# A gated linear recurrence with a causal convolution behind it: 1024-token chunks, word transposes, another split of the engines, and an order written out in full

## The chip, the cores and the metric

The kernel runs on one core of one Trainium2 chip. The metric is the device time of a run in microseconds; the figure for the kernel before is the median of three runs. Besides these runs there is one profiled execution of it, from which every duration below comes.

## What is computed

The inputs `x`, `r_gate` and `i_gate` are float32 of 4 x 6336 x 256 (batch, time, channel). The reference, cut to what matters:

```python
a_base = 1 / (1 + exp(-a_param))
sig_r, sig_i = sigmoid(r_gate), sigmoid(i_gate)
a_t = exp(8.0 * sig_r * log(clip(a_base, 1e-6, 1 - 1e-6)))
x_gated = sqrt(maximum(1 - a_t * a_t, 1e-6)) * sig_i * x
for t in range(S):                       # a recurrence along time, per channel
    h = a_t[:, t] * h + x_gated[:, t]
    y[:, t] = h
gate_pre = sum(conv_w[k] * y_shifted_by(4 - k) for k in range(5))   # causal, per channel
out = (sigmoid(gate_pre) * (y @ w_val)) @ w_out                     # 256 x 256 weights
```

The output is float32, 4 x 6336 x 256. In all, 104 MB go over the DMA queues.

## The kernel before

The 25,344 tokens are cut into windows of 512 (the last has 256). For each window, three loads on SP's queue bring r, i and x in token order (tokens on the partitions, 256 channels in each row; a partition gets four rows of 1 KB that lie 128 tokens apart). The window then passes through these steps; L numbers are lines of the kernel before:

- `tanh` (ACT, L240) makes tanh(r/2) and tanh(i/2), both gates in one instruction, into `tri`, in bf16. Sigmoids are expressed by tanh.
- `u2` (DVE, L246) makes (tanh + 1) * x, the gated input without the norm, into `uring`, still in token order.
- `srT` (PE, L228) transposes the r gate in bf16 blocks of 128 x 128, so that channels lie on the partitions and time runs along the columns. `exp` (ACT, L257, once for each half h of the channels) turns it into a_t in `aring`.
- `e` (POOL, L262) squares a_t into `ering`. `sq` (ACT, L277) takes the square root for several windows at once, since the square root lives in another activation table than tanh and exp; each change costs an ACT_TABLE_LOAD.
- `uT` (PE, L228) transposes the gated input, `xg` (DVE, L290) multiplies it by the norm, in channel order, from PSUM and SBUF into SBUF.
- `scan` (DVE, L306) runs the recurrence along 512 columns for each h into `yring`; POOL copies the last four columns of the window before in front of it (L304), for the convolution.
- `conv` (PE, L321) is a matmul with a diagonal 128 x 128 matrix for each of five taps and two halves; `tg` (ACT, L327) its tanh; `val` (PE, L338) is y @ w_val; `gv` (DVE, L344) makes (tg + 1) * val; `out` (PE, L356) multiplies by w_out, back in token order; `osb` copies PSUM to SBUF on DVE (L367) or ACT (L369); `store` writes out from SP's queue (L373).

The order of issue comes from `make_plan`, a planner that holds a cost and a priority for each step, places each step on its engine at the earliest time that its inputs allow, and sorts the steps by that time. Each engine then executes its instructions in that order, and SP its loads and stores in that order: a store that waits for its copies holds the loads behind it. Buffers: three windows of input, eleven of a_t, squares and u, seven of y. PSUM holds two banks' worth each of `gp` and `val`, and smaller tiles for the transposes and the output.

## Time and profile before

| quantity | value |
|---|---|
| median of 3 runs | 376.22 us (373.58 to 376.86) |
| span of the profiled execution, first to last instruction | 372.5 us |
| mean granted TensorE clock | 0.942 |
| busy: DVE / ACT / PE / POOL | 334.6 / 312.4 / 272.4 / 138.3 us |
| moved by DMA | 104.42 MB, mean 280 GB/s |
| packets between 512 B and 2 KB | nearly all of 105,160 |
| table loads on ACT | 27 of 1.283 us |

The page gives no time of the profiled execution beside its span; the difference to the median, 3.7 us, is what lies around the span. A busy share is the time in which an engine has an instruction under way, averaged over the whole span, so it has to be read by stretches. A group's line names the source line, the engine, the operation, output and input tiles with their sizes, the number of instructions, their busy time, the mean duration in ns, and the idle time of the engine just before them, with what ended it. An idle engine costs something only where others wait for it.

### The profile page before, as it was taken

Reading aid. Unit: us, or ns where it says so; the run is one execution under the profiler, and the core shown is the slowest. Engines: PE = TensorE matmul, PEld = TensorE weight load, DVE = VectorE, ACT = ScalarE, POOL = GpSimd, SP = SyncE. Lnnn points to the kernel's source line nnn. Section 1 sums busy time; section 2 is a strip of 40 time slices with the busy share of each in tenths; the row PEclk is TensorE's granted clock in tenths of the full one; section 3 lists DMA queues with packets and bytes.
Section 4 is the critical chain, followed back from the end, with each engine's and each line's share of the span. In section 5 each row is a group of like instructions: output and inputs, shape, how many; then the busy total and the mean of one; then the engine's idle time right before and its main releaser. Section 6 shows DMA issues by size and latency. Waiting matters only on the chain.

```text
span 372.5 us, 5299 instructions
## 1 busy us (share of the span) xinstructions
PE 272.4 (73%) x1933; PEld 159.9 (43%) x1933; DVE 334.6 (90%) x326; ACT 312.4 (84%) x298; POOL 138.3 (37%) x111
## 2 busy tenths in 40 slices
PE   0362779877686969877677887696976696869994
PEld 0232445444445535434344454363543363435543
DVE  3363999999999979999999999999999999999982
ACT  4898899999998799998967989789997997873342
POOL 2234435634362726434425324451655056300000
PEclk9995699999899899999889989789999899999998
DMA  8999996999999989996889979979999895313333
GB/s 210 355 348 353 356 350 201 298 353 339 345 361 324 330 268 361 352 364 202 280 264 339 351 226 295 356 255 344 301 323 336 278 340 187 127 56 114 113 114 141
DMA packets 105160, 104.42 MB, mean 280 GB/s; under 512 B 3240, under 2 KB 105135, under 8 KB 105135
## 3 DMA queue, kind: packets, MB, share of 16 engines
q1 hardware_dynamic: 104590, 103.83, 85.7%
q0 software_dynamic: 544, 0.26, 0.5%
q8 instruction: 15, 0.25, 0.3%
q14 instruction: 11, 0.08, 0.1%
HBM read 78.39 MB, written 25.95 MB: 280 GB/s over the span
## 4 chain that ended last, share of the span: by engine, by line
DVE 34%; ACT 23%; issue 19%; PE 14%; DMA 5%; POOL 2%; DVEq 0%; ACTq 0%
DVE yring L306 13%; DVE uring L246 8%; DVE gv L344 7%; ACT tri L240 6%; ACT ering L277 5%; PE gp L321 5%; PE ops L356 4%; ACT aring L257 4%; DMA xt<-in_x_dram 3%; DVE xg L290 3%; PE val L338 3%; ACT tg L327 3%; DVE osb L367 2%; ACT L327 2%; ACT L277 2%
## 5 line engine op out<-in xcount | busy, mean ns | idle before, releaser
L262 POOL TENSOR_TENSOR ering<-aring 128x1024 f32<-128x1024 f32 (+1 forms) x50 | 105.7, 2121 | 140.9 <-ACT aring L257 121.8
L321 PE MATMUL gp<-yring,diag 128*128 128x512 bf16 (+4 forms) x530 | 124.5, 384 | 24.7 <-DVE yring L306 14.2
L306 DVE TENSOR_TENSOR_SCAN yring<-aring,yring,xg 128x512 bf16<-128x512 f32 (+4 forms) x98 | 139.5, 1464 | 0.7
L240 ACT ACTIVATE tri<-ri 128x2048 bf16<-128x2048 f32 (+1 forms) x50 | 94.4, 1907 | 0.0
L321 PEld LDWEIGHTS <-diag 128*128 128x128 bf16 x530 | 50.8, 102 | 83.5 <-issue 16.3
L356 PE MATMUL ops<-wo,gv 128*128 128x256 bf16 x396 | 61.8, 280 | 26.2 <-DVE gv L344 12.4
L257 ACT ACTIVATE aring<-srT,khf 128x512 f32<-128x512 bf16 (+1 forms) x100 | 71.8, 791 | 3.4 <-PE srT L228 2.2
L246 DVE SCALAR_TENSOR_TENSOR uring<-tri,xt 128x1024 bf16<-128x1024 bf16 (+1 forms) x50 | 67.4, 1356 | 7.0 <-ACT tri L240 6.9
L327 ACT ACTIVATE tg<-gp 128x1024 bf16<-128x1024 f32 (+1 forms) x50 | 51.1, 1023 | 25.7 <-PE gp L321 21.2
L344 DVE SCALAR_TENSOR_TENSOR gv<-tg,val 128x1024 bf16<-128x1024 bf16 (+1 forms) x50 | 59.7, 1194 | 2.5 <-PE val L338 1.7
L304 POOL COPY yring<-yring 128x8 bf16<-128x8 bf16 x49 | 31.6, 644 | 77.4 <-DVE yring L306 77.4
L356 PEld LDWEIGHTS <-gv 128*128 128x128 bf16 x396 | 36.7, 99 | 50.0 <-DVE gv L344 20.2
L338 PE MATMUL val<-yring,wv 128*128 128x512 bf16 (+4 forms) x212 | 52.1, 371 | 5.3 <-DVE gv L344 5.3
L228 PE MATMUL srT<-ident_b,tri 128*128 128x128 bf16 x396 | 33.4, 232 | 22.2 <-ACT tri L240 22.2
L277 ACT ACTIVATE ering<-ering,b 128x3072 bf16<-128x3072 f32 (+2 forms) x21 | 47.0, 2280 | 0.1
L369 ACT COPY osb<-ops 128x512 f32<-128x512 f32 x46 | 27.2, 592 | 22.2 <-PE ops L356 19.1
L367 DVE COPY osb<-ops 128x512 f32<-128x512 f32 x53 | 36.1, 682 | 9.2 <-PE ops L356 8.0
L228 PE MATMUL uT<-ident_b,uring 128*128 128x128 bf16 x396 | 33.3, 232 | 15.0 <-DVE xg L290 14.7
L228 PEld LDWEIGHTS <-tri 128*128 128x128 bf16 x396 | 27.0, 104 | 33.2 <-ACT tri L240 27.1
L290 DVE TENSOR_TENSOR xg<-uT,ering 128x1024 bf16<-128x1024 bf16 (+1 forms) x50 | 33.7, 675 | 6.2 <-ACT ering L277 6.2
L228 PEld LDWEIGHTS <-uring 128*128 128x128 bf16 x396 | 28.3, 104 | 20.0 <-issue 14.3
L338 PEld LDWEIGHTS <-wv 128*128 128x128 bf16 x212 | 19.9, 99 | 18.9 <-issue 6.6
(31 smaller groups left out, 53.3 us busy)
## 6 DMA issues: line engine op xcount, KB each, us to landing
ri<-in_r_gate_dram SPq DMA_DIRECT2D x49, 512.0 KB, 6.1
ri<-in_i_gate_dram SPq DMA_DIRECT2D x49, 512.0 KB, 7.4
xt<-in_x_dram SPq DMA_DIRECT2D x49, 512.0 KB, 7.3
out_dram<-osb SPq DMA_DIRECT2D x49, 512.0 KB, 4.6
ri<-in_r_gate_dram SPq DMA_DIRECT2D x1, 256.0 KB, 7.0
ri<-in_i_gate_dram SPq DMA_DIRECT2D x1, 256.0 KB, 7.2
xt<-in_x_dram SPq DMA_DIRECT2D x1, 256.0 KB, 6.6
out_dram<-osb SPq DMA_DIRECT2D x1, 256.0 KB
```

The lines of the kernel that those rows point to most:

```text
L228: nc.tensor.transpose(out=dst[:, h, j * P:(j + 1) * P], in_=src[:, j, h * P:(h + 1) * P], identity=ident_b[:])
L240: nc.scalar.activation(out=tri[:, :, 0:nj, :], in_=ri[:, :, 0:nj, :], func=ACT.Tanh, scale=0.5)
L246: nc.vector.scalar_tensor_tensor(out=uring[:, g % NS, 0:nj, :], in0=tri[:, 1, 0:nj, :], scalar=1.0, in1=xt[:, 0:nj, :], op0=ALU.add, op1=A ...
L257: nc.scalar.activation(out=aring[:, g % NS, h, 0:ntok[g]], in_=srT[:, h, 0:ntok[g]], func=ACT.Exp, scale=khf[:, h:h + 1], bias=khf[:, h:h ...
L262: nc.gpsimd.tensor_tensor(out=ering[:, g % NS, :, 0:ntok[g]], in0=a, in1=a, op=ALU.mult)
L277: nc.scalar.activation(out=nring[:, sl:sl + k, 0:H * WIN], in_=ering[:, sl:sl + k].rearrange("p s h t -> p s (h t)"), func=ACT.Sqrt, scale ...
L306: nc.vector.tensor_tensor_scan(out=yb[:, h, o:o + c1 - c0], data0=aring[:, g % NS, h, c0:c1], data1=xg[:, h, c0:c1], initial=0.0 if fresh ...
L321: nc.tensor.matmul(out=gp[:, h, c0:c1], lhsT=diag[:, h, kk, :], rhs=yb[:, h, o:o + c1 - c0], start=(kk == 0), stop=(kk == CONV_K - 1))
L327: nc.scalar.activation(out=tg[:, :, 0:ntok[g]], in_=live.pop(("gp", g))[:, :, 0:ntok[g]], func=ACT.Tanh, scale=0.5)
L338: nc.tensor.matmul(out=val[:, m, c0:c1], lhsT=wv[:, hk, m * P:(m + 1) * P], rhs=yb[:, hk, o:o + c1 - c0], start=(hk == 0), stop=(hk == H - 1))
L344: nc.vector.scalar_tensor_tensor(out=gv[:, :, 0:ntok[g]], in0=live.pop(("tg", g))[:, :, 0:ntok[g]], scalar=1.0, in1=live.pop(("val", g))[: ...
L356: nc.tensor.matmul(out=ops[:, e, :], lhsT=gv[:, hk, p0:p0 + P], rhs=wo2[:, hk, :], start=(hk == 0), stop=(hk == H - 1))
```

## The change

Windows of 512 tokens are grouped in chunks of 1024 (smaller ones at both ends). Each partition now loads four tokens that follow each other, so one piece of 4 KB. tanh writes tokens in pairs, two bf16 values of one channel side by side, and a transpose moves such a pair as one 32-bit word: `tr` for the r gate, `nt` for the norm, `xt` for the gated input. The norm is brought to token order (`nt`), multiplied with u there (`xg`, from PSUM and SBUF), and the product is transposed (`xt`); the scan reads it from PSUM, over the 1024 columns of a chunk. u is made on POOL for most windows, in two instructions (`up`: add one in place, then multiply by x), and on DVE for seven early ones (`uv`). Squares run on POOL (`sq`), six early ones on DVE (`sv`). y lies in one ring of 3096 columns in which each chunk follows on the last, without the copies of four columns. The convolution uses 64 x 64 diagonal blocks, four matmuls for each tap. Weights come by ACT's DMA queue and are cast on POOL. The order of all steps is a written list instead of the planner's. The diff, cut to its core (lr, li and lx are loads; th is tanh, ex exp, rt the square root, sc the scan, cv the convolution, vl val, ou the output matmul, cd and ca its copy on DVE and ACT, st the store):

```diff
--- before
+++ after
-WIN = 512
-NS = 11
-NY = 7
-NIN = 3
-NTRI = 3
-NOSB = 3
-def make_plan(frac):
...
+CHUNKS = [[256], [512], [512, 512], [512, 512],
...
+    512], [512, 512], [512, 512], [512, 512], [512, 512], [512, 512], [512, 512], [512], [256], [256]]
+BATCHES = [[0], [1], [2], [3, 4, 5], [6, 7, 8], [9, 10, 11], [12, 13, 14], [15, 16, 17], [18, 19, 20], [21, 22, 23],
+    [24, 25, 26], [27]]
+NA = 5120
+NE = 5120
+NY = 3096
+NU = 10
+NRI = 4
+NX = 4
+NTRI = 3
+NXG = 2
+NTG = 2
+NGV = 2
+NOSB = 3
+ORDER = """
+s_small s_ident lr.0 li.0 lr.1 li.1 lx.0 lx.1 lr.2 li.2 th.0 li.3 lr.3 s_kt tr.0 li.4 uv.0 th.1 s_diag ex.0.1 tr.1
+li.5 uv.1 s_wload sq.0.1 lx.2 lr.4 lr.5 ex.0.0 th.2 sv.0.0 ex.1.1 li.6 lr.6 th.3 up.2 ex.1.0 tr.2 li.7 lr.7 th.4
+lx.3 lx.4 sq.1.0 ex.2.1 li.8 lr.8 sq.1.1 lx.5 th.5 sv.2.1 lx.6 s_wcast ex.2.0 li.9 lr.9 rt.1 sv.2.0 uv.3 rt.2 uv.4
+lx.7 rt.0 th.6 nt.0 xg.0 xt.0 tr.3 sc.0.1 sc.0.0 uv.5 th.7 lr.10 uv.6 lx.8 ex.3.1 tr.4 lr.11 li.10 lx.9 ex.3.0
...
+gv.46 ou.45.1 tg.47 sc.26.1 ou.46.0 cd.45.1 vl.47 st.45 nt.50 gv.47 cv.48 xg.50 ou.46.1 tg.48 cd.46.0 vl.48 ca.46.1
+ou.47.0 gv.48 st.46 ou.47.1 cv.49 ca.47.1 cd.47.0 xt.27 tg.49 vl.49 sc.27.0 st.47 ou.48.0 sc.27.1 ou.48.1 gv.49
+cv.50 ca.48.1 cd.48.0 vl.50 tg.50 ou.49.0 st.48 gv.50 ca.49.0 ou.50.0 st.49 ca.50.0 st.50
+"""
-            nc.sync.dma_start(dst, src[t0:t0 + nj * P, :].rearrange("(j p) d -> p j d", p=P))
+            nc.sync.dma_start(dst, flat[which][wstart[w]:wstart[w] + n, :].rearrange("(p j) d -> p j d", p=P))
...
+        nc.scalar.preload_act_table_set("natural_log_exp_and_others")
...
+        diag = const.tile([P, H, CONV_K, 64], BF16, name="diag")
...
+        def rot():
+            return psum.tile([P, 512], FP32, name="rot", tag="rot", bufs=4)
...
-            nc.scalar.activation(out=tri[:, :, 0:nj, :], in_=ri[:, :, 0:nj, :], func=ACT.Tanh, scale=0.5)
+        def op_th(w):
+            nq = wins[w] // (2 * P)
+            ri, tri = riring[:, w % NRI], tring[:, w % NTRI]
+            if nq == 2:
+                src = ri.rearrange("p g (q two) d -> p (g q) two d", two=2)
+                dst = tri.rearrange("p g q d two -> p (g q) two d")
+            else:
+                src, dst = ri[:, :, 0:2, :], tri[:, :, 0, :, :].rearrange("p g d two -> p g two d")
+            nc.scalar.activation(out=dst, in_=src, func=ACT.Tanh, scale=0.5)
+        def u_args(w):
+            nq = wins[w] // (2 * P)
+            return (uring[:, w % NU, 0:nq].rearrange("p q d two -> p q two d"),
+                    tring[:, w % NTRI, 1, 0:nq].rearrange("p q d two -> p q two d"),
+                    xring[:, w % NX, 0:2 * nq, :].rearrange("p (q two) d -> p q two d", two=2))
+        def op_up(w):
+            u, t1, xt = u_args(w)
+            flat_t = tring[:, w % NTRI, 1, 0:wins[w] // (2 * P)].rearrange("p q d two -> p (q d two)")
+            nc.gpsimd.tensor_scalar(out=flat_t, in0=flat_t, scalar1=1.0, scalar2=None, op0=ALU.add)
+            nc.gpsimd.tensor_tensor(out=u, in0=t1, in1=xt, op=ALU.mult)
+        def op_uv(w):
+            u, t, xt = u_args(w)
+            for q in range(wins[w] // (2 * P)):
+                nc.vector.scalar_tensor_tensor(out=u[:, q], in0=t[:, q], scalar=1.0, in1=xt[:, q],
+                                               op0=ALU.add, op1=ALU.mult)
+        def op_tr(c):
+            for h in range(H):
+                bank = rot()
+                for w in cwins[c]:
+                    nq = wins[w] // (2 * P)
+                    o = (wstart[w] - cstart[c]) // 2
+                    for q in range(nq):
+                        nc.tensor.transpose(
+                            out=bank[:, o + q:o + wins[w] // 2:nq],
+                            in_=tring[:, w % NTRI, 0, q, h * P:(h + 1) * P, :].rearrange("p d two -> p (d two)")
+                            .bitcast(FP32),
+                            identity=ident[:])
+                live["rT", c, h] = bank
+        def op_ex(c, h):
+            bank = live.pop(("rT", c, h))
+            nc.scalar.activation(out=aring[:, h, a_at[c]:a_at[c] + clen[c]],
+                                 in_=bank[:].bitcast(BF16)[:, 0:clen[c]], func=ACT.Exp,
+                                 scale=khf[:, h:h + 1], bias=khf[:, h:h + 1])
+        def squares(c, h):
+            return ering[:, h, e_at[c]:e_at[c] + clen[c]], aring[:, h, a_at[c]:a_at[c] + clen[c]]
+        def op_sq(c, h):
+            e, a = squares(c, h)
+            nc.gpsimd.tensor_tensor(out=e, in0=a, in1=a, op=ALU.mult)
+        def op_sv(c, h):
+            e, a = squares(c, h)
+            nc.vector.tensor_tensor(out=e, in0=a, in1=a, op=ALU.mult)
-        def op_u2(g, eng, n):
-            nj = ntok[g] // P
-            xt, tri = live.pop(("xt", g)), live["tri", g]
-            nc.vector.scalar_tensor_tensor(out=uring[:, g % NS, 0:nj, :], in0=tri[:, 1, 0:nj, :], scalar=1.0,
-                                           in1=xt[:, 0:nj, :], op0=ALU.add, op1=ALU.mult)
+        def op_rt(b):
+            cs = BATCHES[b]
+            k = 0
+            while k < len(cs):
+                m = k + 1
+                while m < len(cs) and e_at[cs[m]] == e_at[cs[m - 1]] + clen[cs[m - 1]]:
+                    m += 1
+                o = e_at[cs[k]]
+                n = e_at[cs[m - 1]] + clen[cs[m - 1]] - o
+                nc.scalar.activation(out=ering[:].bitcast(BF16)[:, :, 2 * o:2 * o + n], in_=ering[:, :, o:o + n],
+                                     func=ACT.Sqrt, scale=-0.25, bias=b025[:, 0:1])
+                for j in range(k, m):
+                    live["n", cs[j]] = (e_at[cs[k]], e_at[cs[j]] - e_at[cs[k]])
+                k = m
+        def op_nt(w):
+            c = chunk_of[w]
+            nq = wins[w] // (2 * P)
+            base, off = live["n", c]
+            o = base + (off + wstart[w] - cstart[c]) // 2
+            bank = rot()
+            for q in range(nq):
+                for h in range(H):
+                    nc.tensor.transpose(out=bank[:, (q * H + h) * P:(q * H + h + 1) * P],
+                                        in_=nwords[:, h, o + q:o + wins[w] // 2:nq], identity=ident[:])
+            live["nT", w] = bank
+        def op_xg(w):
+            nq = wins[w] // (2 * P)
+            nc.vector.tensor_tensor(out=xgring[:, w % NXG, 0:nq].rearrange("p q d two -> p (q d two)"),
+                                    in0=live.pop(("nT", w))[:, 0:nq * D].bitcast(BF16),
+                                    in1=uring[:, w % NU, 0:nq].rearrange("p q d two -> p (q d two)"), op=ALU.mult)
+        def op_xt(c):
+            for h in range(H):
+                bank = rot()
+                for w in cwins[c]:
+                    nq = wins[w] // (2 * P)
+                    o = (wstart[w] - cstart[c]) // 2
+                    for q in range(nq):
+                        nc.tensor.transpose(
+                            out=bank[:, o + q:o + wins[w] // 2:nq],
+                            in_=xgring[:, w % NXG, q, h * P:(h + 1) * P, :].rearrange("p d two -> p (d two)")
+                            .bitcast(FP32),
+                            identity=ident[:])
+                live["xT", c, h] = bank
+        def op_sc(c, h):
+            xT = live.pop(("xT", c, h))[:].bitcast(BF16)
+            for s, (o0, o1, fresh, col) in enumerate(segs[c]):
+                if fresh and h == 0:
+                    nc.vector.memset(yring[:, :, col - 4:col], 0.0)
+                if fresh:
+                    first = 0.0
+                elif s == 0 and y_wrap[c]:
+                    e = live["yend", c - 1]
+                    if h == 0:
+                        nc.vector.tensor_copy(out=yring[:, :, 0:4], in_=yring[:, :, e - 4:e])
+                    first = yring[:, h, e - 1:e]
+                else:
+                    first = yring[:, h, col - 1:col]
+                nc.vector.tensor_tensor_scan(out=yring[:, h, col:col + o1 - o0],
+                                             data0=aring[:, h, a_at[c] + o0:a_at[c] + o1],
+                                             data1=xT[:, o0:o1], initial=first, op0=ALU.mult, op1=ALU.add)
+                live["yend", c] = col + o1 - o0
+        def op_cv(w):
+            gp = psum.tile([P, H, 512], FP32, name="gp", tag="gp", bufs=1)
+            for a, b, col in pieces(w):
+                for k in range(CONV_K):
+                    for h in range(H):
+                        for half in range(2):
+                            oh = half if h == 0 else 1 - half
+                            nc.tensor.matmul(out=gp[oh * 64:oh * 64 + 64, h, a:b],
+                                             lhsT=diag[half * 64:half * 64 + 64, h, k, :],
+                                             rhs=yring[half * 64:half * 64 + 64, h, col - 4 + k:col - 4 + k + b - a],
+                                             start=(k == 0), stop=(k == CONV_K - 1))
+            live["gp", w] = gp
+        def op_tg(w):
+            nc.scalar.activation(out=tgring[:, w % NTG, :, 0:wins[w]], in_=live.pop(("gp", w))[:, :, 0:wins[w]],
+                                 func=ACT.Tanh, scale=0.5)
-        def op_xg(g, eng, n):
-            xg = work.tile([P, H, WIN], BF16, name="xg", tag="xg", bufs=2)
-            nh = nring[:, g % NS, 0:H * WIN].rearrange("p (h t) -> p h t", h=H)
-            nc.vector.tensor_tensor(out=xg[:, :, 0:ntok[g]], in0=live.pop(("uT", g))[:, :, 0:ntok[g]],
-                                    in1=nh[:, :, 0:ntok[g]], op=ALU.mult)
-            live["xg", g] = xg
-        def op_scan(g, eng, n):
-            xg = live.pop(("xg", g))
-            yb = yring[:, g % NY]
-            py = yring[:, (g - 1) % NY]
-            pend = ntok[g - 1] + 4 * len(segs[g - 1]) if g else 0
-            for s, (c0, c1, fresh) in enumerate(segs[g]):
-                o = c0 + 4 + 4 * s
-                if fresh:
-                    nc.gpsimd.memset(yb[:, :, o - 4:o], 0.0)
-                else:
-                    nc.gpsimd.tensor_copy(out=yb[:, :, o - 4:o], in_=py[:, :, pend - 4:pend])
-                for h in range(H):
-                    nc.vector.tensor_tensor_scan(
-                        out=yb[:, h, o:o + c1 - c0],
-                        data0=aring[:, g % NS, h, c0:c1],
-                        data1=xg[:, h, c0:c1],
-                        initial=0.0 if fresh else py[:, h, pend - 1:pend],
-                        op0=ALU.mult, op1=ALU.add,
-                    )
-        def op_conv(g, eng, n):
-            yb = yring[:, g % NY]
-            gp = psum.tile([P, H, WIN], FP32, name="gp", tag="gp", bufs=1)
-            for h in range(H):
-                for s, (c0, c1, fresh) in enumerate(segs[g]):
-                    for kk in range(CONV_K):
-                        o = c0 + 4 * s + kk
-                        nc.tensor.matmul(out=gp[:, h, c0:c1], lhsT=diag[:, h, kk, :], rhs=yb[:, h, o:o + c1 - c0],
-                                         start=(kk == 0), stop=(kk == CONV_K - 1))
-            live["gp", g] = gp
...
+        def op_ou(w, i):
+            J = wins[w] // P
+            gv = gvring[:, w % NGV]
+            ops = rot()
+            for e in range(2):
+                j = 2 * i + e
+                for hk in range(H):
+                    nc.tensor.matmul(out=ops[:, e * D:(e + 1) * D], lhsT=gv[:, hk, j:wins[w]:J], rhs=wo[:, hk, :],
+                                     start=(hk == 0), stop=(hk == H - 1))
+            live["ops", w, i] = ops
+        def copy(w, i, eng):
+            dst = oring[:, w % NOSB, 2 * i:2 * i + 2, :].rearrange("p j d -> p (j d)")
+            src = live.pop(("ops", w, i))[:]
+            if eng == "D":
+                nc.vector.tensor_copy(out=dst, in_=src)
+            else:
+                nc.scalar.copy(out=dst, in_=src)
+        def op_cd(w, i):
+            copy(w, i, "D")
-                    nc.tensor.matmul(out=ops[:, e, :], lhsT=gv[:, hk, p0:p0 + P], rhs=wo2[:, hk, :],
-                                     start=(hk == 0), stop=(hk == H - 1))
...
-        for (t, op, i, eng, n) in plan:
-            ops_by_name[op](i, eng, n)
+        for word in ORDER.split():
+            name, *idx = word.split(".")
+            emit[name](*[int(k) for k in idx])
```

## The prediction, made before the changed kernel had run

> **What bounds the kernel now.** I read the page first: busy times, then the slices.
>
> ```profile
> span 372.5 us, 5299 instructions
> PE 272.4 (73%) x1933; PEld 159.9 (43%) x1933; DVE 334.6 (90%) x326; ACT 312.4 (84%) x298; POOL 138.3 (37%) x111
> ...
> DVE  3363999999999979999999999999999999999982
> ACT  4898899999998799998967989789997997873342
> ...
> DMA  8999996999999989996889979979999895313333
> GB/s 210 355 348 353 356 350 201 298 353 339 345 361 324 330 268 361 352 364 202 280 264 339 351 226 295 356 255 344 301 323 336 278 340 187 127 56 114 113 114 141
> ```
>
> DVE is at 9 from the fifth slice nearly to the end. The sums by stretch say how tightly (columns: length, busy time and count of PE, PEld, DVE, ACT, POOL; clock; DMA share; GB/s):
>
> ```profile
> 0.00:40.00 40.00, 13.79 (x95) 9.09 (x96) 19.19 (x32) 32.90 (x29) 11.94 (x15) 0.87 1.03 320
> 40.00:320.00 280.00, 216.94 (x1569) 127.47 (x1568) 272.03 (x249) 255.50 (x243) 123.15 (x86) 0.95 0.95 307
> 320.00:372.00 52.00, 41.69 (x274) 23.31 (x272) 43.34 (x47) 23.98 (x28) 3.25 (x11) 0.99 0.31 107
> ```
>
> Between 40 and 320 us DVE idles 8 us of 280 (2.9%), ACT 24.5 (8.8%): DVE bounds that stretch. Its 38 us of idle time lie at the start (21) and the end (9). DMA is next: 95% busy, and no slice moves more than 364 GB/s.
>
> Next, what fills DVE:
>
> ```profile
> L262 POOL TENSOR_TENSOR ering<-aring 128x1024 f32<-128x1024 f32 (+1 forms) x50 | 105.7, 2121 | 140.9 <-ACT aring L257 121.8
> ...
> L306 DVE TENSOR_TENSOR_SCAN yring<-aring,yring,xg 128x512 bf16<-128x512 f32 (+4 forms) x98 | 139.5, 1464 | 0.7
> L240 ACT ACTIVATE tri<-ri 128x2048 bf16<-128x2048 f32 (+1 forms) x50 | 94.4, 1907 | 0.0
> ...
> L246 DVE SCALAR_TENSOR_TENSOR uring<-tri,xt 128x1024 bf16<-128x1024 bf16 (+1 forms) x50 | 67.4, 1356 | 7.0 <-ACT tri L240 6.9
> ...
> L344 DVE SCALAR_TENSOR_TENSOR gv<-tg,val 128x1024 bf16<-128x1024 bf16 (+1 forms) x50 | 59.7, 1194 | 2.5 <-PE val L338 1.7
> ```
>
> These means hide two populations. The timeline of DVE, then that of POOL:
>
> ```profile
> 155.21 2.45 DVE L306 TENSOR_TENSOR_SCAN yring<-aring,yring,xg 128x512 bf16<-128x512 f32 x2
> ...
> 164.95 5.75 DVE L306 TENSOR_TENSOR_SCAN yring<-aring,yring,xg 128x512 bf16<-128x512 f32 x2
> ```
>
> ```profile
> 164.97 4.66 POOL L262 TENSOR_TENSOR ering<-aring 128x1024 f32<-128x1024 f32 x2 [2.15 <-ACT aring L257]
> ```
>
> The same pair of scans takes 2.45 us while POOL is quiet and 5.75 beside POOL's squares. Setting every instruction of the trace against L262: of the 512-column scans, 61 without overlap average 1.26 us, 31 with it 2.05. Over a clean 1.235 us the scans lose 27 us, and L246, over 1.21, 8 us. L344 (1.20 clean, 1.21 overlapped) and L290 (0.68 both) lose nothing. What separates them: scan and L246 read two SBUF tensors, L344 and L290 one SBUF and one PSUM tensor.
>
> **The change, part by part.** A window is 512 tokens; there are 49.5.
>
> DVE. (a) The gated input u leaves DVE for 44 of 51 windows. That removes 67.4 us; seven windows stay, as 13 half instructions at the 512-column row's 0.68: 8.8. (b) Scans run over 1024 columns with the input in PSUM. From the clean rows (0.739 at 256, 1.235 at 512, so about 0.5 per 256) 1024 columns cost 2.2 to 2.3; I take 2.3: 46 x 2.3 + 4 x 1.25 + 6 x 0.74, and 1 for sequence cuts, is 116. This takes L344's and L290's rows as proof that an operand in PSUM keeps POOL away; if not, see rivals. (c) The product with the norm keeps one PSUM and one SBUF operand: 48 x 0.68 + 3 x 0.42 = 33.9. gv: 48 x 1.204 + 3 x 0.68 = 59.8. Copies rise from 53 to 75: 75 x 0.682 = 51.2. Six squares at the start, 5,376 columns at gv's 1.18 ns: 6.3. Sum 276, against 334.6.
>
> ACT. tanh 48 x 1.925 + 3 x 1.06 = 95.6; its output is now written as pairs, with a stride, which no row has: between nothing and, if strided writes halved the rate, another 90; I take nothing, as the read side is unchanged. exp: rows 0.562 (256) and 0.795 (512) give 1.26 for 1024; 46 x 1.26 + 4 x 0.795 + 6 x 0.562 = 64.6 (71.8 before). sqrt: 0.839 ns a column (1.136 at 1024, 2.854 at 3072) over 50,688 columns plus 14 x 0.277 = 46.4. tg 51.3. Copies 24 x 0.592 = 14.2. The order list has nine stays in the sqrt table, so 18 loads x 1.283 = 23.1. Sum 295, against 312.4; four more loads lie before the first data.
>
> POOL. L304's 50 small copies vanish (31.6), since the state columns now follow each other in one ring. Squares 45,312 columns at the clean 1.89 per 1024: 84. Added is u in two instructions. Add-one, one input, 1024 columns: from 0.95 (the identity's memset, 0.205 for 128 columns against 0.1 for one) to 1.89 (a two-input pass). Multiply: 1.89 clean to 2.87 (slowest L262). So 43 x 2.84 = 122 up to 43 x 4.76 = 205; I take 122, the clean rows, because DVE's steady work no longer reads two SBUF operands. POOL: 206 (289 at worst), all beside ACT; 289 would stand level with ACT and cost some 15 us of waits. POOL now also frees the x buffers, so a late u delays the next lx on SP's queue, and the loads behind it.
>
> The Trainium skill, GPSIMD Engine Reference, section "Engine selection", speaks against this part: elementwise two-input work belongs on VectorE, being about twice as slow on GpSimd. The rows agree on the slowness (L262's 1.89 against 1.20); but leaving u on DVE by that rule would make DVE 276 + 59 = 335, as before.
>
> PE. Its streams step 0.055 us per bf16 transpose, and 0.22 per 512-column matmul:
>
> ```profile
> 350.29 0.61 PE L228 MATMUL uT<-ident_b,uring 128*128 128x128 bf16 x8
> 350.74 2.33 PE L321 MATMUL gp<-yring,diag 128*128 128x512 bf16 x10
> ...
> 355.17 0.39 PE L228 MATMUL uT<-ident_b,uring 128*128 128x128 bf16 x4
> ```
>
> (0.61 - 0.39 for four; 2.33 less one latency for nine.) A window now costs 16 x 0.055 + 10 x 0.216 + val 0.86 + out 0.88 = 4.8. Afterwards: 12 f32 word transposes instead of 16, from 0.055 to 0.26 each (the setup's f32 weight loads took 0.20, added unhidden): 0.66 to 3.1; I take 0.11, double width: 1.3. The convolution is 20 matmuls of 64x64, 512 columns: 1.08 if four run together, 4.32 if none do; no row shows overlap, so I take two at a time, today's 2.16. Sum 5.2 a window, 257 us, hidden under ACT's 295. The Trainium skill, TensorEngine Tiling (Array Packing), section "Restrictions and Gotchas", says that different row tiles cannot access the same PSUM bank at once; here both halves of one h write one bank. By that rule, two at a time: 257; by its four independent tiles 1.08, so 203. Both are hidden.
>
> DMA. The same 104.4 MB in pieces of 4 KB. 1 KB packets took 46 ns (median), 4 B packets 9: at that slope 4 KB takes 157 ns, or 417 GB/s; with no gain, 356. So 293 down to 250 us; I take the middle, some 385 GB/s and 271, not binding. Loads still queue on SP behind stores that wait for copies, as L373 does today.
>
> The sum. ACT has most, but the end belongs to DVE: counting the order list after the last tanh (th.50), ACT has 32 us left and DVE 43.7 (scans 19.4, gv 14.6, xg 4.9, copies 4.8). So: first tanh at 7.5 (8.9 now, its first loads halved), ACT's work through th.50 262.5, DVE's rest 43.7, last matmul, copy and store 3.5: 317.2. Stalls: today's bound engine idles 2.9%, the engine below it 8.8%. With ACT, DVE and DMA within 10% of one another I take 4% of 306: 12.2. Span 329.4. The page gives no time beside the profiled execution's span; the median of 376.22 stands 3.7 over it, and I add that: 333. From 2.9% to 8.8%, 330 to 348.
>
> **The rivals.**
> (1) DMA takes DVE's place: 4 KB pieces gain nothing. The order list puts 91 MB ahead of the last tanh's input, 255.5 us at 356 GB/s, 269 at today's 95% share. 1.5 + 269 + 24.5 (ACT from there to th.50) + 43.7 + 3.5 + 5 of waits = 347; time 351. For it: 95% busy now, at most 364 GB/s. Against it: the 9 ns floor of a packet.
> (2) The change doesn't free DVE: scans with PSUM input still meet POOL. With POOL's two-input work twice as long, the 27 us become 53: DVE 329, plus today's 38 idle, 367; time 371. Against it: 42 overlapped L344 and L290 instructions without loss.
> (3) The slower side: PE becomes the bound, because 64x64 matmuls run one after another and f32 transposes take 0.155, midway. 4.32 + 1.74 + 1.87 = 7.9 a window, 392, plus 15 at the ends: 407; time 411. It decides from 7.2 us a window. For it: no row shows two matmuls at once. Against it: both must fail; serial tiles with 0.055 transposes give 6.7 a window, which is faster than today.
>
> **How the numbers follow.** Forecast 0.62, rival 1 0.17, rival 2 (with POOL near its 289) 0.10, rival 3 0.08, something unlisted 0.03. The time is the forecast's, 333. The range runs from 316 (no stalls at all gives 321; 5 us less if the clean rows are undercut) to 360, past rival 1. A measurement of this kernel tells about 1% from no change; faster takes the forecast, rival 1 and most of rival 2: 0.89; same 0.03, slower 0.08.
>
> **What would show it.** Right: 1024-column scans near 2.3 us whatever POOL does; DVE near 276 and ACT near 295 busy, neither idle over 10% between 40 us and the last tanh; POOL's u near 2.8 a window; PE under 260. Wrong: scans of 3 us; tanh idle behind DMA (rival 1); conv matmuls stepping 0.2 each, with gp waits ahead of tg (rival 3); tanh much over 1.93.

## The result, and the profile after

The changed kernel takes 396.86 us (median of 4 runs, 395.18 to 398.37) against 376.13 for the kernel before on the same chip: a ratio of 1.058, 95% interval 1.053 to 1.063. It is 20.7 us slower; the forecast was 333. The first lines of the page of the changed kernel, with the slices of three engines:

```profile
span 395.4 us, 5990 instructions
PE 264.5 (67%) x2289; PEld 174.0 (44%) x2289; DVE 275.5 (70%) x277; ACT 311.2 (79%) x220; POOL 309.5 (78%) x147
...
DVE  1214573588698664987868643999689957958985
ACT  6598979559999659976998666888899698875553
POOL 0081499929999999999999999999999999690100
```

DVE is relieved as forecast (275.5 us, forecast 276). But POOL, at 138 us before, is now at 309.5, and its row of slices is the one that DVE's was before: a 9 nearly throughout. The stretch from 40 to 320 us (columns as in the first stretch table: length, then PE, PEld, DVE, ACT, POOL):

```profile
40.00:320.00 280.00, 195.82 (x1675) 127.92 (x1673) 208.75 (x205) 230.88 (x143) 264.47 (x114) 0.89 0.79 286
```

POOL is busy 264.5 of 280 us, ACT 230.9, DVE 208.8. POOL bounds the kernel. What fills it, from the groups of the page:

```profile
L286 ACT ACTIVATE tring<-riring 128x2048 bf16<-128x2048 f32 (+1 forms) x51 | 124.3, 2453 | 28.3 <-POOL uring L298 25.5
L297 POOL TENSOR_SCALAR tring<-tring 128x1024 bf16<-128x1024 bf16 (+1 forms) x44 | 120.3, 2735 | 9.7 <-ACT tring L286 9.7
L298 POOL TENSOR_TENSOR uring<-tring,xring 128x1024 bf16<-128x1024 bf16 (+1 forms) x44 | 102.4, 2326 | 16.5 <-DMA xring<-in_x_dram 12.9
...
L331 POOL TENSOR_TENSOR ering<-aring 128x1024 f32<-128x1024 f32 (+2 forms) x50 | 85.6, 1731 | 33.6 <-ACT aring L322 33.4
```

Adding one in place (L297) is POOL's dearest group: 2.74 us a window, more than the multiply with two inputs (L298). The gates' tanh (L286) has 2.45 us instead of 1.9, and before it lies ACT's largest wait for another engine: 25.5 us, for L298 to free the gate buffers.

What the change was meant to do at DVE, it did. The scans over 1024 columns, from the groups kept apart by shape, and the 20 matmuls of a convolution, from PE's timeline:

```profile
L402 DVE TENSOR_TENSOR_SCAN yring<-aring,yring,rot 128x1024 bf16<-128x1024 f32 x40 | 91.9, 2332 | 6.0 <-PE rot L381 6.0
```

```profile
166.74 1.28 PE L414 MATMUL gp<-yring,diag 64*64 64x512 bf16 x20
```

Of the 40 scans, 37 overlap POOL's work and average 2.33 us; the three others average 2.34. The 20 matmuls start in five groups of four, 0.22 to 0.24 us apart; within a group the starts lie 3 to 4 ns apart.

### The profile page after: what moved, and what is told of

Its sections match the earlier page's. It is cut to its first block, busy times and chain, and to the rows that moved or that the text cites. A ratio compares the mean times of both kernels' runs of the same rounds, so it can differ in the third digit from the quotient of the medians.

```text
span 395.4 us, 5990 instructions
## 1 busy us (share of the span) xinstructions
PE 264.5 (67%) x2289; PEld 174.0 (44%) x2289; DVE 275.5 (70%) x277; ACT 311.2 (79%) x220; POOL 309.5 (78%) x147
## 5 line engine op out<-in xcount | busy, mean ns | idle before, releaser
L286 ACT ACTIVATE tring<-riring 128x2048 bf16<-128x2048 f32 (+1 forms) x51 | 124.3, 2453 | 28.3 <-POOL uring L298 25.5
L297 POOL TENSOR_SCALAR tring<-tring 128x1024 bf16<-128x1024 bf16 (+1 forms) x44 | 120.3, 2735 | 9.7 <-ACT tring L286 9.7
L298 POOL TENSOR_TENSOR uring<-tring,xring 128x1024 bf16<-128x1024 bf16 (+1 forms) x44 | 102.4, 2326 | 16.5 <-DMA xring<-in_x_dram 12.9
L402 DVE TENSOR_TENSOR_SCAN yring<-aring,yring,rot 128x1024 bf16<-128x1024 f32 (+5 forms) x54 | 108.9, 2047 | 7.8 <-PE rot L381 7.8
L331 POOL TENSOR_TENSOR ering<-aring 128x1024 f32<-128x1024 f32 (+2 forms) x50 | 85.6, 1731 | 33.6 <-ACT aring L322 33.4
L414 PE MATMUL gp<-yring,diag 64*64 64x512 bf16 (+7 forms) x1080 | 69.3, 387 | 17.4 <-ACT tgring L421 17.2
L322 ACT ACTIVATE aring<-rot,khf 128x1024 f32<-128x1024 bf16 (+2 forms) x56 | 59.4, 1107 | 21.6 <-PE rot L313 16.7
L445 PE MATMUL rot<-wo,gvring 128*128 128x256 bf16 x396 | 62.7, 293 | 15.7 <-ACT aring L322 5.9
L364 PE MATMUL rot<-ident,ering 128*128 128x128 f32 x198 | 38.9, 326 | 49.5 <-ACT ering L350 40.8
L434 DVE SCALAR_TENSOR_TENSOR gvring<-tgring,val 128x1024 bf16<-128x1024 bf16 (+1 forms) x51 | 60.3, 1181 | 15.1 <-PE val L429 9.9
L453 DVE COPY oring<-rot 128x512 f32<-128x512 f32 x75 | 49.8, 681 | 20.4 <-PE rot L445 15.1
L370 DVE TENSOR_TENSOR xgring<-rot,uring 128x1024 bf16<-128x1024 bf16 (+1 forms) x51 | 33.4, 665 | 37.7 <-issue 22.6
L421 ACT ACTIVATE tgring<-gp 128x1024 bf16<-128x1024 f32 (+1 forms) x51 | 50.7, 993 | 10.8 <-PE gp L414 10.6
L364 PEld LDWEIGHTS rot<-ident,ering 128*128 128x128 f32 x198 | 30.3, 209 | 59.8 <-ACT ering L350 43.3
```

The costliest lines, as they stand in the source:

```text
L286: nc.scalar.activation(out=dst, in_=src, func=ACT.Tanh, scale=0.5)
L297: nc.gpsimd.tensor_scalar(out=flat_t, in0=flat_t, scalar1=1.0, scalar2=None, op0=ALU.add)
L298: nc.gpsimd.tensor_tensor(out=u, in0=t1, in1=xt, op=ALU.mult)
L331: nc.gpsimd.tensor_tensor(out=e, in0=a, in1=a, op=ALU.mult)
L364: nc.tensor.transpose(out=bank[:, (q * H + h) * P:(q * H + h + 1) * P], in_=nwords[:, h, o + q:o + wins[w] // 2:nq], identity=ident[:])
L402: nc.vector.tensor_tensor_scan(out=yring[:, h, col:col + o1 - o0], data0=aring[:, h, a_at[c] + o0:a_at[c] + o1], data1=xT[:, o0:o1], initi ...
```

## The experiments

Three theories stood at the start. A: POOL's add-one is the cause, since it puts POOL's total above ACT's. B: ACT's tanh with a strided side is what decides. C: a third part is the written order, laid out for other durations than these. Line numbers can shift by one where a kernel drops a line. "Before" is the kernel before, run on the same chip each time.

**e1_no_add: theory A by subtraction.** The add-one is left out, so the output differs.

```diff
 def op_up(w):
-    nc.gpsimd.tensor_scalar(out=flat_t, in0=flat_t, scalar1=1.0, scalar2=None, op0=ALU.add)
     nc.gpsimd.tensor_tensor(out=u, in0=t1, in1=xt, op=ALU.mult)
```

> POOL's add-one (L297, 120 us busy) is left out, so u is tanh * x instead of (tanh + 1) * x; all else stays. Theory A (POOL bounds the changed kernel, because add-one takes 2.77 us a window and not 0.95 to 1.89): POOL busy falls from 309.5 to about 190, ACT (311) becomes the bound, time 335 to 355. Theory B (ACT bounds it, because the pair-wise tanh takes 2.52 instead of 1.93): time stays over 385. Theory C (the written order is at fault: engines wait on one another because it was made for other durations): time stays over 376.

Measured: 370.2 us (four runs, 365.1 to 371.0), ratio 0.979 (0.967 to 0.991). So 26.7 us, give or take some 3, of the changed kernel's time hang on the add-one, and without it the kernel is not slower than before. From its page, and its stretches 100 to 160 and 160 to 220 us:

```profile
PE 253.1 (70%) x2289; PEld 170.3 (47%) x2289; DVE 275.0 (76%) x277; ACT 309.5 (85%) x220; POOL 190.5 (52%) x103
```

```profile
100.00:160.00 60.00, 46.28 (x432) 31.49 (x432) 52.83 (x54) 59.85 (x37) 44.36 (x22) 0.97 0.93 342
160.00:220.00 60.00, 44.99 (x419) 31.11 (x416) 47.42 (x51) 59.67 (x38) 43.41 (x21) 0.94 0.91 350
```

POOL falls by 119 us, and ACT takes its place: 59.85 of 60 us. A is the largest part, but 370 lies outside the band of 335 to 355 that A gave, and far from 333.

**e2_u_all_dve and e3_u_12_dve: the part undone, whole and by a quarter.** u goes back to DVE for all 44 windows, or for twelve (9, 12, ... 42).

```diff
-... th.3 up.2 ex.1.0 ...
+... th.3 uv.2 ex.1.0 ...
```

> Undoes one part: u is made on DVE for all windows, at the same places of the order. POOL keeps the squares alone (about 85 us), DVE goes from 275 to about 337 (43 windows at 1.45) plus what it loses to POOL's squares. Theory A: DVE is the bound again, 365 to 395, so the move of u to POOL is what the change lost by. Theory B: 395 or more. Theory C: 385 or more.

> 12 of the 44 windows of u (every third, 9 to 42) go from POOL to DVE. Theory A: POOL 309 - 12 x 5.14 = 248, DVE 275 + 12 x 1.45 and some lost to POOL = 295 to 305, ACT 311 is the highest, time 340 to 355, better than both kernels. Theory B: no change from 397. Theory C: above 376.

Measured: 409.06 (ratio 1.090, 1.081 to 1.098) and 376.14 (1.002, 0.998 to 1.006). With twelve, POOL has 251.8 and DVE 297.5, and the loss of 20.7 us is gone, but A's 340 to 355 is not reached. With all 44, where A allowed 395 at most, DVE has 339.4, some 5 more than before the change, yet idles 67 us of a span of 406.4 where the kernel before idled 38. The same engine as bound and nearly the same work give 33 us more: the first sign that this order fits badly when the durations are others.

**e4_tanh_rows: theory B.** tanh writes plain rows instead of pairs of tokens (the output differs); all else stays.

```diff
-                src = ri.rearrange("p g (q two) d -> p (g q) two d", two=2)
-                dst = tri.rearrange("p g q d two -> p (g q) two d")
...
+            src = ri[:, :, 0:2 * nq, :].rearrange("p g j d -> p g (j d)")
+            dst = tri[:, :, 0:nq].rearrange("p g q d two -> p g (q d two)")
```

> tanh writes its output in rows instead of pairs (the values then stand at other places, all shapes and later steps are the same). ACT falls by about 29 us (2.52 back to 1.93 for 48 windows). Theory A: ACT isn't the bound, time 393 to 401. Theory B: time falls by 20 to 29, to about 370. Theory C: between the two.

Measured: 391.27, ratio 1.043 (1.038 to 1.047). ACT falls from 311.2 to 284.3 us and the time by 5.6: the 27 us are there, but behind POOL they hardly count (A had 393 to 401, C the stretch between A and B). B falls as the main cause.

**e5_units: the disputed costs alone.** A kernel of three repeats of each operation, with nothing else of the computation in it.

```diff
+nc.gpsimd.tensor_scalar(out=t1, in0=t1, scalar1=1.0, scalar2=None, op0=ALU.add)
...
+nc.gpsimd.tensor_tensor(out=b1[:], in0=t1, in1=ones[:], op=ALU.add)
...
+nc.gpsimd.tensor_copy(out=b1[:], in_=t1)
```

> Computes nothing of the reference: it times the disputed instructions alone, three of each, 1024 columns on POOL (2048 for tanh on ACT), no other engine working on SBUF. POOL add-one in place on bf16 should repeat 2.77. Theory P1 (any one-input tensor-scalar pass costs that, about 2.5 ns a column): out of place, float32 and multiply all 2.5 to 2.8, while a two-input add of a tile of ones takes 1.9 to 2.4. Theory P2 (in place, or bf16 on both sides, costs extra): the out-of-place or the float32 form takes 1.0 to 1.9. tanh: rows 1.93, pairs written with a stride 2.5. Theory W (the strided 2-byte write costs it): pairs written in order, read with a stride of a row, take 1.93 again. Rival R (any strided side costs it): 2.5 too. DVE's add-one on 1024 bf16: 0.4 to 0.5.

From its groups (the columns are as before; `pairw` is written by tanh in pairs, `pairr` read in pairs and written in order, `rows` plain):

```profile
L54 POOL TENSOR_SCALAR pairw<-pairw 128x1024 bf16<-128x1024 bf16 x3 | 8.3, 2773 | 24.9 <-ACT pairw L48 24.7
...
L57 POOL TENSOR_SCALAR f<-xt 128x1024 f32<-128x1024 f32 x3 | 8.3, 2773 | 0.2
...
L48 ACT ACTIVATE pairw<-ri 128x2048 bf16<-128x2048 f32 x3 | 7.3, 2448 | 0.0
L60 POOL TENSOR_TENSOR b<-pairw,xt 128x1024 bf16<-128x1024 bf16 x3 | 7.0, 2341 | 0.0
...
L49 ACT ACTIVATE pairr<-ri 128x2048 bf16<-128x2048 f32 x3 | 7.0, 2326 | 0.0
...
L58 POOL TENSOR_TENSOR b<-pairw,ones 128x1024 bf16<-128x1024 bf16 x3 | 6.3, 2113 | 0.0
L47 ACT ACTIVATE rows<-ri 128x2048 bf16<-128x2048 f32 x3 | 5.7, 1898 | 0.0
...
L62 POOL COPY b<-pairw 128x1024 bf16<-128x1024 bf16 x3 | 3.1, 1037 | 0.0
```

Without any neighbour, POOL's tensor-scalar pass takes 2.77 us whatever its type, operation or place; with a tile of ones as second input the same sum takes 2.11, a copy 1.04. So it is no contention and no matter of bf16: this form of instruction is slow. The tanh costs 1.90 in order, 2.45 with a strided write and 2.33 with a strided read, so theory W, by which only the write costs, falls. The multiply of u (L60) takes 2.34 here too, so its price in the changed kernel is no contention either.

**e6_add_dve, e7_add_dve_pairs, e8_store_later: repairs.** e6 makes the add-one on DVE, the multiply stays on POOL. e7 also lets tanh read the pairs with a stride and write in order. e8 also moves the first store (st.0) in the order to just ahead of st.1.

```diff
-            nc.gpsimd.tensor_scalar(out=flat_t, in0=flat_t, scalar1=1.0, scalar2=None, op0=ALU.add)
+            nc.vector.tensor_scalar(out=flat_t, in0=flat_t, scalar1=1.0, scalar2=None, op0=ALU.add)
```

```diff
-                src = ri.rearrange("p g (q two) d -> p (g q) two d", two=2)
-                dst = tri.rearrange("p g q d two -> p (g q) two d")
+                src = ri.rearrange("p g (q two) d -> p (g q) d two", two=2)
+                dst = tri.rearrange("p g q d two -> p (g q) d two")
```

```diff
-... cd.0.0 xt.2 st.0 lr.14 ... cd.1.1 xt.4 st.1 ...
+... cd.0.0 xt.2 lr.14 ... cd.1.1 xt.4 st.0 st.1 ...
```

> The add-one of u moves from POOL to DVE (one instruction of about 0.45 us a window, in place), the multiply stays on POOL; the output is the reference's. POOL falls to about 190, DVE rises to about 295, ACT 311 stays highest. Theory A (POOL's add-one was the bound, ACT is next): 365 to 375, like the kernel without the add. Rival (DVE's add-one waits for POOL's reads, up to 2.4 us each, and holds the queue): 385 or more.

> As e6_add_dve, and tanh walks its elements in the order of the pairs, so that the strided side is the read and the write is in order. Under theory W tanh returns to 1.93, ACT falls from 311 to about 282, DVE (295) becomes the highest: 12 to 25 us less than e6_add_dve, 345 to 360. Under rival R nothing changes against e6_add_dve.

> As e7_add_dve_pairs, and the first store (st.0) is moved in the order list from before the loads of window 14 to just before st.1. In the changed kernel this store sits on SP's queue from 61 to 72 us and ACT then waits 8.7 us for a transposed gate. If the store holds the loads and these hold ACT: 5 to 10 us less than e7_add_dve_pairs. If the loads would have waited for their buffers anyway: the same within 1%.

Measured: 370.2 (ratio 0.985, 0.980 to 0.989), 368.16 (0.980, 0.975 to 0.985), 366.9 (0.975, 0.971 to 0.980). e6 costs DVE 11 us and brings all of e1's gain. e7 is 2.0 us below e6, where theory W had 12 to 25: the read with a stride saves ACT 5 us and no more (305.6 against 310.6). The store was not what held up the start of the kernel: in e8 ACT still waits 9.1 us at 75 to 84 us for PE's transposes.

**e9_swap_words: why PE was late there.** PE's timeline in e8, then ACT's:

```profile
63.31 1.03 PE L445 MATMUL rot<-wo,gvring 128*128 128x256 bf16 x4 [3.01 <-DVE gvring L434]
64.14 0.42 PE L364 MATMUL rot<-ident,ering 128*128 128x128 f32 x1
70.22 0.92 PE L364 MATMUL rot<-ident,ering 128*128 128x128 f32 x3 [5.67 <-ACT ering L350]
```

```profile
64.75 5.42 ACT L350 ACTIVATE ering<-ering,b 128x6144 bf16<-128x6144 f32 x1
```

The four L364 are `nt.3`, the norm of window 3, which belongs to chunk 2; its square root was done at 38 us. The first of them ran at 64.14. The other three started when the square root of chunks 3 to 5 (`rt.3`, written just ahead of `nt.3` in the order) ended at 70.17. The second transpose is the first to read the other half of the channels. `op_rt` writes both halves with one strided instruction, and between its first and its last column lie the columns that this transpose reads. The edit exchanges the two words; no engine's own sequence changes.

```diff
-ou.0.0 up.10 rt.3 nt.3 cv.1 ...
+ou.0.0 up.10 nt.3 rt.3 cv.1 ...
```

> e8_store_later with two words of the order exchanged: nt.3 now stands before rt.3 instead of behind it. No engine's own sequence changes (nt.3 is TensorE's, rt.3 ScalarE's); only which of the two is written first. In e8 the first of nt.3's four transposes started at 64.14 us and the other three at 70.22, the moment at which ScalarE's square roots of rt.3 (64.75 to 70.17) ended, although window 3 belongs to chunk 2, whose norm was done at 38 us, and rt.3 covers chunks 3 to 5. Theory W (a needless wait: because rt.3's write covers both feature halves in one strided region, a transpose of the second half written after it is held until it ends): TensorE's wait of 5.7 us at 64 to 70 us goes, the following products, scans, transposes and exponentials move forward, ScalarE's 9.1 us wait at 75 to 84 us shrinks to 3 to 5, and the time falls by 3 to 7 us from e8's 366.9, to 360 to 364. Rival N (the wait is the norm's own and only looks early, or the ramp is held by the loads): 366 to 368, and ScalarE's wait at 75 to 84 stays at 9 us.

Measured: 360.48, ratio 0.958 (0.954 to 0.961), so 6.4 us for two words. From PE's timeline:

```profile
63.75 0.64 PE L364 MATMUL rot<-ident,ering 128*128 128x128 f32 x4
```

All four now run without a break, and ACT's wait for the next transposed gate, 9.1 us in e8, becomes 2.0. ACT's timeline in e8, then in e9:

```profile
83.90 1.21 ACT L322 ACTIVATE aring<-rot,khf 128x1024 f32<-128x1024 bf16 x1 [9.13 <-PE rot L313]
```

```profile
77.72 1.21 ACT L322 ACTIVATE aring<-rot,khf 128x1024 f32<-128x1024 bf16 x1 [1.96 <-PE rot L313]
```

That the wait was needless, and its price, are shown; that it comes from one range laid over both halves is the reading that fits which of the four waited.

**e10_new_order: theory C.** e9's steps in another order, from the casting of the weights on; three output copies go from DVE to ACT and one square from DVE to POOL. The words were moved one by one as long as a plan with the measured durations became shorter. The add-one got a word of its own (`ad`).

```diff
-... nt.1 vl.0 up.7 ex.4.0 ...
+... sc.0.0 li.9 ad.7 nt.1 tr.4 th.8 up.7 li.11 ...
```

> The instructions of e9_swap_words (add-one on VectorE, multiply on GpSimd, tanh with a strided read) in another written order from the casting of the weights on: list moved word by word, with the durations that these runs measured (multiply 2.35, tanh 2.38, scan 2.33, exp 1.19, add-one 0.41, squares 1.89 a window or half chunk) and the needless waits counted; of the output copies 72 are on VectorE and 27 on ScalarE instead of 75 and 24; of the squares 51 on GpSimd and 5 on VectorE instead of 50 and 6. Busy times by engine should stay within 3 us of e8's: ScalarE 306, VectorE 286, GpSimd 189, TensorE 250 to 256. Theory C (what is left of the gap to the forecast is stalls that the order of the change carries, because it was laid out for other durations): ScalarE's idle time, 59 of 364 us in e8, falls to 30 to 40, and the time to 338 to 352. Rival S (the stalls are those of the dependences themselves: a chain scan to scan, the ramp, the end; an order can't move them): 358 to 366, at most 3 us below e9.

Measured: 356.2, ratio 0.948 (0.944 to 0.953). It beats both kernels and is the fastest here that leaves nothing out, 5.2% faster than before. But it is 4.3 us below e9, neither C's figure nor its rival's, and ACT still idles 46.7 us.

**e11_no_add_rows and e12_no_add_rows_order: the order without the two mis-sized terms.** Both leave out the add-one and write plain rows, the edits of e1 and e4 together (the output differs): e11 in the order of the change, e12 in e10's, where the line that falls away is VectorE's add-one. The core of e11's diff:

```diff
-                src = ri.rearrange("p g (q two) d -> p (g q) two d", two=2)
+            src = ri[:, :, 0:2 * nq, :].rearrange("p g j d -> p g (j d)")
...
-            nc.gpsimd.tensor_scalar(out=flat_t, in0=flat_t, scalar1=1.0, scalar2=None, op0=ALU.add)
```

> The changed kernel with the add-one left out and the gates' tanh writing plain rows, in the order of the change (the output differs in both). With both mis-sized terms of the forecast taken out, the busy totals should be those that it assumed or less: ScalarE 283 (311 less the 27 that e4 took off), VectorE 275, GpSimd 190, TensorE 253. Theory L (the two terms and the needless wait are the whole error, and the stalls are as small as forecast): the largest total, 283, with the forecast's start, end and 4% of stalls, 7.5 + 3.5 + 12, gives a span of 306 and a time of 310. Theory C (the order itself carries a third term, of 30 us or more): e1's span of 363 falls only by what ScalarE's full stretches, 100 to 220 us, give back at 10% less work, 8 to 14 us, to 349 to 355 and a time of 352 to 360.

> The same work as e11_no_add_rows (no add-one, rows) in the order of e10_new_order (the output differs in both). Theory C, second part: what e10's order took off beside e8's, 10.7 us of 366.9, comes off here too, so 340 to 350 where e11 has 352 to 360, and ScalarE's idle time is 45 to 55 us, most of it in the first 40 and the last 40 us. Rival S (with no engine near its limit the order does not matter): within 3 us of e11. If both kernels lie above the forecast of 333 with every engine's total at or below what the forecast assumed, the forecast's stalls, 12 us, were too small whatever the other terms.

Measured: 358.94 (0.958, 0.951 to 0.966) and 335.39 (0.891, 0.883 to 0.900). The busy times, e11's and then e12's:

```profile
PE 254.6 (71%) x2289; PEld 169.7 (48%) x2289; DVE 275.5 (77%) x277; ACT 283.6 (79%) x220; POOL 190.6 (53%) x103
```

```profile
PE 246.7 (74%) x2289; PEld 163.8 (49%) x2289; DVE 268.5 (80%) x273; ACT 283.7 (85%) x223; POOL 191.6 (57%) x104
```

The same steps, but for the three copies and the square that e10 gave to other engines, and 23.5 us between them (e12 was expected at 340 to 350, and did better). ACT, which has the most work, has the same total in both and idles 73.3 us in e11, 50.7 in e12. The granted TensorE clock differs as well (0.921 and 0.964 in the profiled executions), but one run of e11 had 0.957 and took 358.9 us, as did runs at 0.914 and 0.921 (359.0, 358.7). C holds: the order is a term of its own.

**e13_order_no_add and e14_order_adds_clear: why e10 had so little of it.** e13 is e10 without the add-one alone (the output differs). e14 has e10's steps in a third order, with as many copies and squares on each engine but not the same ones, laid out with the rule that an add-one begun beside an instruction of POOL lasts until that one ends.

```diff
 def op_ad(w):
-    flat_t = tring[:, w % NTRI, 1, 0:wins[w] // (2 * P)].rearrange("p q d two -> p (q d two)")
-    nc.vector.tensor_scalar(out=flat_t, in0=flat_t, scalar1=1.0, scalar2=None, op0=ALU.add)
+    pass
```

> e10_new_order with the add-one left out and nothing else (the output differs); tanh keeps its strided read, 22 us of ScalarE above plain rows. Theory H (VectorE's add-ones, 30.9 us of busy time in e10, of which 14 are held beside GpSimd's instructions, eat the order's gain): 337 to 346, and VectorE 262 to 268 busy. Rival T (it is ScalarE's tanh that keeps e10 from e12's 335): 351 to 356, little below e10's 356.2.

> The instructions of e10_new_order in another order, laid out with one rule more: an add-one on VectorE that would start while GpSimd has an instruction under way lasts until that one ends. Counts are e10's (72 output copies on VectorE and 27 on ScalarE, 51 squares on GpSimd and 5 on VectorE). By the list only 2 add-ones should be held, against 14 found in e10's trace. Theory H: the add-ones' busy time falls from 30.9 us to 18 to 23, VectorE's from 294 to 284 to 288, and the time from 356.2 to 344 to 352. Rival (the hold is off the path, or the real times drift so far from the list's that as many are held again): 354 to 358.

Measured: e13 344.91 (0.917, 0.911 to 0.923), e14 360.14 (0.959, 0.954 to 0.965). So in the new order the add-one costs 11.3 us, and the strided tanh the 9.5 between e13 and e12. The rule behind e14 is seen in e10, DVE's timeline first, then POOL's:

```profile
185.51 0.42 DVE L297 TENSOR_SCALAR tring<-tring 128x1024 bf16<-128x1024 bf16 x1
...
187.22 1.48 DVE L297 TENSOR_SCALAR tring<-tring 128x1024 bf16<-128x1024 bf16 x1
188.62 4.57 DVE L405 TENSOR_TENSOR_SCAN yring<-aring,yring,rot 128x1024 bf16<-128x1024 f32 x2
```

```profile
186.06 2.36 POOL L301 TENSOR_TENSOR uring<-tring,xring 128x1024 bf16<-128x1024 bf16 x1 [10.44 <-DMA out_dram<-oring]
188.78 2.43 POOL L301 TENSOR_TENSOR uring<-tring,xring 128x1024 bf16<-128x1024 bf16 x1 [0.36 <-DVE tring L297]
```

The add-one of 185.51 finds POOL at rest and takes 0.42 us. That of 187.22 finds a multiply that ends at 188.42, and ends itself at 188.70, 0.28 later. The scans behind it run beside the next multiply at their usual 2.3 each. Of e10's 42 add-ones of full width, 26 begin with POOL at rest and average 0.41 us; 16 begin with an instruction of POOL under way and average 1.16. In e9, whose POOL mostly waits for the add-one, these are 36 and 6 (0.55). e14 was a miss: where its list had 2, 18 add-ones began beside POOL's work (1.31 on average), DVE rose to 300.7 us, and it lost e10's gain. ACT also has two more table loads there, 24 against 22. That the hold exists is shown, and that the add-one costs 11.3; how much of that is the hold is not, since an order that avoids it was not found.

## Why the prediction was wrong, point by point

**What was right.** DVE's total, 275.5 against 276, and its large terms: scans 115.8 (forecast 116), gv 60.3 (59.8), copies 49.8 (51.2), xg 33.4 (33.9). The small terms were too low: u 11.1 (8.8), squares 8.2 (6.3), and 7.6 for eight copies of eight columns, which had no term. These groups add up to 286; that instructions of different groups overlap by some 10 us made the total fit, which is luck. A scan with its input in PSUM is untouched by POOL (2.33 us beside it, 2.34 alone; forecast 2.3), so rival 2 fell. 4 KB packets took 159 ns in the median (forecast 157) and a slice moved up to 412 GB/s, so rival 1 fell. (Its 91 MB are in fact MiB: the order list puts some 95 MB ahead of the last tanh, which would have put the rival near 363.) PE stood at 264.5, beside a forecast of 257, by errors that cancel: the convolution's group has 69 us where 107 were allowed, since the 64 x 64 tiles run four at a time, 20 in 1.28 us; the groups of the f32 transposes have 106 where 64 were, though the median step is the 0.11 to 0.12 us that was taken. Rival 3 fell with that: PE is not the bound. The one thing rival 3 had right, "slower", came from elsewhere. The rule that the prediction quoted from the Trainium skill, TensorEngine Tiling (Array Packing), section "Restrictions and Gotchas", that different row tiles cannot access one PSUM bank at once, does not hold here: two row tiles write each bank, in different partitions, and all four run together.

**The step that failed first: POOL's term.** The add-one was bounded by 0.95 and 1.89 us, from a memset and from a two-input pass, on the assumption that one input can't cost more than two. It took 2.74 to 2.77: outside both bounds. The multiply took 2.33, inside its own (1.89 to 2.87), but the lower end was chosen: the row of 1.89 is a square, whose two inputs are one tile, and with two tiles e5 has 2.34 without any neighbour. So u cost 5.1 us a window, not 2.84, and POOL 309.5 us: above the 206 of the sum and above the 289 called the worst, which was to cost "some 15 us". Only 206 went into the forecast, and no rival had POOL as the bound, though the profile had no row of this instruction. The Trainium skill, GPSIMD Engine Reference, section "Engine selection", did speak against two-input work there. But it calls one-input work on GpSimd roughly line-rate, and this one-input form was the dearest thing on the engine (2.77 in e5, a copy 1.04).

**The second: tanh.** Between nothing and 90 us were named, and nothing was taken, "as the read side is unchanged". It was 29 us on ACT (2.45 against 1.90 in e5), and the prediction's own sign of being wrong, "tanh much over 1.93", came true. Behind POOL it hid (e4: 5.6 us); with POOL relieved it is worth 11.3 (e1 to e11).

**The third: the stalls.** 4% of 306 us were allowed, read from engines whose order the planner had made with fitting costs. The new order is a fixed list, and no row showed how it would run. The lag it carries is 23.5 us (e11 to e12). One needless wait, worth 6.4 us from e8 to e9, is in e11 as well: three transposes of nt.3 start there at 69.70 us, when the square roots of rt.3 end.

The three close the account, as far as subtractions in one order of taking away can:

| step | us |
|---|---|
| the changed kernel | 396.9 |
| without the add-one on POOL (e1) | -26.7 |
| with plain rows from tanh (e11) | -11.3 |
| in another order (e12) | -23.5 |
| e12 | 335.4 |
| forecast | 333 |

The first two steps can shift against each other by some 3 us, as e1's runs lie between 365.1 and 371.0. The agreement of the last two lines owes something to luck: in e12 ACT has 283.7 us of work, 11 less than the forecast gave it, and idles 50.7 of a span of 334.4, where the forecast (295 in 329.4) left 34.

**What stays open.** The idle time in e12 that no order tried here removed, which waits make up the 23.5 us, and whether an order exists in which the add-one on DVE always falls between POOL's instructions. A version in which the add-one disappears from DVE and POOL with the output kept was not tried.

## What to carry to other kernels

An operation that the profile has no row for, placed on an engine in the middle of every window, needs a run of its own before the sum is made: e5 takes 100 us of chip time, and with its durations the prediction's own sums give POOL some 304 us and ACT some 320 (an estimate: 84 + 43 x 5.11, and 295 + 48 x 0.525), not 206 and 295. Bounds taken from "fewer inputs, so cheaper" are no bounds, and where an upper bound makes an engine level with the leader, that engine is a rival with a price. A written order is part of a kernel's cost model: when one duration changes it has to be laid out anew, and when a wait looks needless, see whether two words of the list can change places.

## What the runs showed of the hardware that was not expected

- GpSimd's tensor-scalar pass takes 2.77 us for 128 x 1024, for f32 and bf16, add and multiply; two-input passes 1.89 (a square) to 2.34 and a copy 1.04.
- ScalarE's tanh over 2048 columns: 1.90 in order, 2.33 with a strided f32 read, 2.45 with a strided bf16 write.
- A bf16 add of a constant on VectorE, 0.42 us alone, ends 0.28 us after the GpSimd instruction that was under way when it began; e5 shows it too, where the add beside GpSimd's copy took 1.23 us and the two others 0.43. In the changed kernel a VectorE copy of eight bf16 columns takes 0.16 us alone and 0.95 to 1.85 beside GpSimd's two-input passes. The Trainium skill, SBUF — State Buffer, section "Who interferes with whom", describes such an exclusive lock between the two engines, held for a whole instruction, and these rows agree with it. The scans with one operand in PSUM show nothing of it (2.33 us beside GpSimd's work, 2.34 without).
- Four 64 x 64 matmul tiles run together, two of them into each PSUM bank, in different partitions: 20 matmuls over 512 columns in 1.28 us.
